# A hash-attention and gated-FFN kernel: batch 1 loaded and prepared early, the 1/32 moved into the copies from PSUM, V casts tied to bits, and a norm moved

## The chip, the core and the metric

The kernel runs on one core of a Trainium2 chip. The metric is the device time of one execution in microseconds (us); of several executions the median is given. TensorE (PE, with its weight loads shown as PEld), VectorE (DVE), ScalarE (ACT), GpSimd (POOL) and SyncE (SP) each work through their own instruction list in order and wait for one another through semaphores. DMAs move data between main memory, SBUF (the on-chip memory) and, here, also from one place of SBUF to another. PE writes its results to PSUM, from which ACT and DVE copy them out.

## The reference, cut to what matters

```python
# q, k, v: (4, 8, 768, 64); proj: (64, 6); x below: (3072, 512)
q_bits, k_bits = (q @ proj > 0), (k @ proj > 0)
mask = bucket(q_bits)[:, :, :, None] == bucket(k_bits)[:, :, None, :]
scores = where(mask, q @ k.T / sqrt(64), -1e9)
attn = softmax(scores)                    # with 1e-9 added to the sum
x = heads_side_by_side(attn @ v)
xn = x / sqrt(mean(x * x) + 1e-6) * rms_g
g = xn @ w_gate
out = (g * sigmoid(g) * (xn @ w_val)) @ w_out
```

A query sees only those keys whose six hash bits equal its own.

## The kernel before, in words

**Mask by arithmetic.** Each pair of heads of a batch has one tile `qk` of 71 rows: rows 0 to 63 hold the head dimensions in f16, scaled by 1/32 (`DIM`), rows 64 to 69 hold the hash bits as +0.5 or -0.5, row 70 a constant. One matmul over 71 rows thus gives score and bit agreement together, and `exp` with scale 128 makes the weight of a pair with unequal bits vanish. The constant rows are written once into each of six rotating `qk` tiles (`const_rows`).

**Preparing a pair of heads** (`make_prep`). `load_qk` and `load_v` issue the DMAs on SP's queue into rings of four buffers. `tr_mm` j transposes q (j = 0, 2) or k (j = 1, 3) on PE, three 128x128 blocks each, into a PSUM tile of the pool `ring` (four buffers); `tr_ev` copies it to SBUF, on ACT for q and DVE for k. `hash_mm` multiplies with proj for all four (query or key, head) combinations, `bits` compares with zero on DVE, and eight `place` DMAs of 4.5 KB, issued by SP, carry the bits to rows 64 to 69 of `qk`. `dims` writes rows 0 to 63, by the engine given ("a", "v" or "p" for GpSimd). The first two pairs of batch 0 (A and Bp; the others are C and Dp) write most bits straight from PSUM (`hash_one`, `direct`). `vcast` turns V into f16 and `vsum` adds up V for the 1e-9 term, both on GpSimd unless said otherwise.

**Attention** (`queue_attention`). u = 0 to 7 counts half-batches: batch u // 2, and the first or second half of its queries. Each u has 24 slots (8 heads of 3 key blocks): two score matmuls, two exponentials on ACT, and, 1.5 slots later, six matmuls with V (`pv`). Every six slots `post` divides by the sums on DVE; it reads the one accumulator tile `pv`, so the next `pv` group waits for it. After slot 23 `sumsq` squares and sums x, one call for each of the three token blocks.

**Norm and FFN**, one half-batch behind attention. `queue_norm`: `rstd` (one DVE operation and a power on GpSimd), `scale` (xn, three DVE operations), then `tr`, twelve f16 transposes on PE in two groups, and two copies to `xnT`, one on DVE and one on ACT. `queue_gates`: twelve blocks of eight matmuls, with tanh on ACT and two multiplications on DVE. `queue_out`: six groups of six matmuls, two half-batches behind attention.

**What sets the order.** Every step is given to `at` with a position, in units of a slot from the start of u = 0, and the list is emitted in order of position (lines 635 and 636). Each engine then sees its own part of that list, in that order, and takes it as its operands become ready: the position is no time, and an engine that is early in its list runs ahead until something that it needs is missing. `base` is the position of the half-batch in which a batch is prepared: 24, 72 and 120 for batches 1, 2 and 3. Pairs 0 and 1 of a batch are prepared in that half-batch, pairs 2 and 3 in the next.

## Time and profile before

| what | value |
|---|---|
| median of 3 runs | 379.11 us (377.8 to 380.17) |
| the profiled execution | 377.56 us |
| its span, first to last instruction | 375.8 us |
| PE busy | 348.1 us, 93% of the span |
| DVE, ACT, POOL busy | 236.6, 241.0, 83.9 us |
| mean clock granted to PE | 0.990 |
| first scores of u=0 | at 11.59 us |
| first output matmul (position 48.15) | at 81.04 us |
| moved by DMA | 31.2 MB, 83 GB/s over the span |

Times are read from the start of the span. Busy time is the union of an engine's instructions; the ends of matmuls are modelled, so a busy PE may still hold short gaps. A wait "A <- B" is time in which A's engine stood idle before A, ended by B. L182 is line 182 of the kernel. All of the prediction's rows are of this one execution.

### The profile page before, as it was taken

Reading aid. Unit: us, or ns where it says so; the run is one execution under the profiler, and the core shown is the slowest. Engines: PE = TensorE matmul, PEld = TensorE weight load, DVE = VectorE, ACT = ScalarE, POOL = GpSimd, SP = SyncE. Lnnn points to the kernel's source line nnn. Section 1 sums busy time; section 2 is a strip of 40 time slices with the busy share of each in tenths; the row PEclk is TensorE's granted clock in tenths of the full one; section 3 lists DMA queues with packets and bytes.
Section 4 is the critical chain, followed back from the end, with each engine's and each line's share of the span. In section 5 each row is a group of like instructions: output and inputs, shape, how many; then the busy total and the mean of one; then the engine's idle time right before and its main releaser. Section 6 shows DMA issues by size and latency. Waiting matters only on the chain.

```text
span 375.8 us, 7954 instructions
## 1 busy us (share of the span) xinstructions
PE 348.1 (93%) x3056; PEld 211.6 (56%) x3056; DVE 236.6 (63%) x475; ACT 241.0 (64%) x548; POOL 83.9 (22%) x106
## 2 busy tenths in 40 slices
PE   4887699999999989999999989999999999997995
PEld 3455366565656646565656646666565656663552
DVE  5776556758566684766746586566837565466670
ACT  3678766676767657676767656776676766872331
POOL 5999765200000292000000083200000000000000
PEclk9999889999999999999999999999999999999999
DMA  7702999900008503200004804200001000200202
GB/s 271 261 3 28 247 276 239 236 4 3 3 5 273 191 5 129 87 3 2 4 4 151 315 2 128 89 5 0 6 3 64 25 0 2 86 2 0 85 2 84
DMA packets 23846, 31.20 MB, mean 83 GB/s; under 512 B 1992, under 2 KB 20608, under 8 KB 23808
## 3 DMA queue, kind: packets, MB, share of 16 engines
q1 hardware_dynamic: 17824, 25.97, 20.5%
q0 software_dynamic: 5824, 4.72, 8.1%
q8 instruction: 24, 0.39, 0.4%
q14 instruction: 14, 0.11, 0.1%
q10 hardware_dynamic: 160, 0.00, 0.0%
HBM read 28.58 MB, written 6.29 MB: 93 GB/s over the span
## 4 chain that ended last, share of the span: by engine, by line
PE 53%; issue 25%; DVE 10%; POOL 5%; DMA 3%; ACT 3%; POOLq 0%; SPq 0%; DVEq 0%; ACTq 0%
PE v_ps L447 12%; PE g_ps L447 11%; PE o_ps L497 9%; PE s_ps L301 9%; PE pv L331 5%; PE trps L182 4%; POOL qk L241 3%; PE hps L195 2%; DVE qk L239 2%; DMA ql<-in_q_dram 2%; DVE sq L360 2%; DVE xn L395 2%; DMA kl<-in_k_dram 1%; ACT p L308 1%; ACT xnT L416 1%
## 5 line engine op out<-in xcount | busy, mean ns | idle before, releaser
L308 ACT ACTIVATE p<-s_ps 128x384 f16<-128x384 f32 x384 | 162.7, 496 | 70.6 <-PE s_ps L301 70.5
L301 PE MATMUL s_ps<-qk 71*128 71x384 f16 x384 | 95.7, 328 | 1.6 <-DVE qk L221 1.2
L464 DVE SCALAR_TENSOR_TENSOR a<-th,g_ps 128x384 f32<-128x384 f32 x96 | 53.1, 554 | 48.9 <-ACT th L456 47.7
L447 PE MATMUL g_ps<-xnT,wg 128*128 128x384 f16 x384 | 79.2, 325 | 4.2 <-ACT xnT L416 2.5
L447 PE MATMUL v_ps<-xnT,wv 128*128 128x384 f16 x384 | 78.0, 326 | 3.2 <-DVE a L464 3.2
L331 PEld LDWEIGHTS <-p 128*128 128x128 f16 x1152 | 60.2, 98 | 30.3 <-issue 8.9
L497 PE MATMUL o_ps<-wo,ht 128*128 128x512 f16 x288 | 68.7, 379 | 0.0
L331 PE MATMUL pv<-v,p 128*128 128x65 f16 x1152 | 67.9, 194 | 0.5
L456 ACT ACTIVATE th<-g_ps 128x384 f32<-128x384 f32 x96 | 47.8, 498 | 20.3 <-PE g_ps L447 17.3
L473 DVE TENSOR_TENSOR ht<-a,v_ps 128x384 f16<-128x384 f32 x96 | 53.0, 552 | 8.2
L388 POOL TENSOR_TENSOR rs<-ms,mhalf 128x3 f32<-128x3 f32 x8 | 6.9, 862 | 225.7 <-DVE ms L384 225.7
L447 PEld LDWEIGHTS <-wv 128*128 128x128 f16 x384 | 37.5, 98 | 29.2 <-issue 4.8
L447 PEld LDWEIGHTS <-wg 128*128 128x128 f16 x384 | 35.2, 97 | 26.1 <-issue 6.7
L497 PEld LDWEIGHTS <-ht 128*128 128x128 f16 x288 | 27.0, 97 | 27.4
L301 PEld LDWEIGHTS <-qk 71*128 71x128 f16 x384 | 28.4, 99 | 9.9 <-issue 1.3
L508 ACT ACTIVATE osb<-o_ps 128x512 f32<-128x512 f32 x23 | 13.7, 598 | 24.8 <-PE o_ps L497 24.8
L191 DVE COPY kT<-trps 128x384 f32<-128x384 f32 x32 | 17.7, 553 | 12.8 <-PE trps L182 12.6
L346 DVE RECIPROCAL r<-pv 128x6 f32<-128x6 f32 x32 | 6.2, 194 | 27.7 <-PE pv L331 27.7
L395 DVE SCALAR_TENSOR_TENSOR xn<-x,rs,grow 128x512 f16<-128x512 f32 x24 | 19.6, 869 | 5.6 <-POOL rs L388 5.6
L182 PE MATMUL trps<-ident,ql 128*128 128x128 f32 x96 | 17.7, 297 | 5.6 <-DMA ql<-in_q_dram 5.6
L189 ACT ACTIVATE qT<-trps 128x384 f32<-128x384 f32 x32 | 15.8, 493 | 10.9 <-PE trps L182 8.6
L182 PE MATMUL trps<-ident,kl 128*128 128x128 f32 x96 | 17.3, 292 | 1.7 <-DMA kl<-in_k_dram 1.4
(55 smaller groups left out, 280.5 us busy)
## 6 DMA issues: line engine op xcount, KB each, us to landing
ql<-in_q_dram SPq DMA_DIRECT2D x16, 384.0 KB
kl<-in_k_dram SPq DMA_DIRECT2D x16, 384.0 KB
vl<-in_v_dram SPq DMA_DIRECT2D x16, 384.0 KB
out_dram<-osb SPq DMA_DIRECT2D x7, 768.0 KB
qk<-bits SPq DMA_DIRECT2D x116, 4.5 KB
wg<-in_moe_w_gate_dram POOLq DMA_DIRECT2D x4, 384.0 KB, 13.6
wv<-in_moe_w_val_dram POOLq DMA_DIRECT2D x4, 384.0 KB, 17.0
wo<-in_moe_w_out_dram POOLq DMA_DIRECT2D x4, 384.0 KB, 24.7
```

The costliest lines, as they stand in the source:

```text
L182: nc.tensor.transpose(m[:, i, :], src[:, i, :], ident)
L189: nc.scalar.activation(dst, mm, AF.Copy)
L191: nc.vector.tensor_copy(dst, mm)
L301: nc.tensor.matmul(s_ps, qk[0:71, 2 + hh, 128 * jt : 128 * jt + 128], qk[0:71, hh, HQ * hf : HQ * hf + HQ], start=True, stop=True,)
L308: nc.scalar.activation(p, s_ps, AF.Exp, scale=SCL)
L331: nc.tensor.matmul(acc[:, t, hh, :], p[:, 128 * t : 128 * t + 128], v16s[b % 2][:, 2 * (jt % 3) + jt // 3, h, :], start=False, stop=(n % 6 ...
L395: nc.vector.scalar_tensor_tensor(out=tl["xn"][:, t, :], in0=x_of[u][:, t, :], scalar=tl["rs"][:, t : t + 1], in1=grow, op0=ALU.mult, op1=A ...
L447: nc.tensor.matmul(ps, w[:, kt, fs], xnT[:, kt, :], start=(kt == 0), stop=(kt == 3))
L456: nc.scalar.activation(th, tl[f][0], AF.Tanh, scale=0.5)
L464: nc.vector.scalar_tensor_tensor(out=a, in0=th, scalar=1.0, in1=g_ps, op0=ALU.add, op1=ALU.mult)
L473: nc.vector.tensor_mul(ht_of[u][f], a, v_ps)
L497: nc.tensor.matmul(tl[t], ht_of[u][f][:, 128 * t : 128 * t + 128], wo[:, f, :], start=(f == 0), stop=(f == 11),)
```

## The change

Seven edits, all to order and form; what is computed stays the same.

- **proj** is loaded once, after ACT's table load and warm-up, and DVE copies it to the other places that need it. A's transposes come in the order q, q, k, k instead of q, k, q, k.
- **The 1/32** is applied when q and k are copied from PSUM (`tr_ev`), on ACT or DVE; `dims` becomes a plain copy on all three engines. The sign of the hash product doesn't change by it.
- **Batch 1 early.** q and k of its pairs 0 and 1 are loaded at positions 1.5 and 4.2 (22 and 27 before), pairs 2 and 3 at 12.5 and 13.5. Pair 0 is prepared from 16.5 (28.4 before), inside u=0, and pair 1 from 32.3 (34.3). Both have all four evictions on DVE. The last two `const_rows` move from 26 and 27 to 12.6 and 12.7.
- **V loads and casts.** For batches 2 and 3 each V load, cast and sum stands after the bits (and so the placements) of a pair: pairs 0 and 1 after the bits of pair 0, pairs 2 and 3 after those of pair 1. For batch 1 they are at 30 to 36.3. Everywhere the hash comes 0.3 slot later.
- **Squares** of u=0 and u=7 are summed in two parts, 384 columns before the last `post` and 128 after it, and the parts added.
- **Norm transposes** come 5.2 slots behind the norm's start in u=0 (8.0 before), 3.7 in the others (4.1) and 5.0 for the last.
- **Around them:** the gates of u=0 start at 31 with a spacing of 1.42 (34.2 and 1.13 before); some bit placements of batch 0 that only the second half of the queries needs go behind others, one eviction of Bp goes to ACT, and the first gate weights are issued at 13.0 and 13.1 (12.1 and 12.2).

```diff
@@ -83,11 +83,10 @@
     pj = const.tile([128, 32], FP32, name="pj")
     nc.vector.memset(pj, 0.0)
-    nc.scalar.dma_start(out=pj[0:64, 0:6], in_=proj)
-    nc.scalar.dma_start(out=pj[64:128, 6:12], in_=proj)
     warm = const.tile([128, 1], FP32, name="warm")
     nc.vector.memset(warm, 0.0)
     nc.scalar.activation(warm, warm, AF.Exp)
+    nc.scalar.dma_start(out=pj[0:64, 0:6], in_=proj)
     ident = const.tile([128, 128], FP32, name="ident")
     make_identity(nc, ident)
     NQK = 6
@@ -112,10 +111,10 @@
     for e in range(2):
         t = const.tile([128, 32], FP32, name=f"pj1_{e}")
         nc.vector.memset(t, 0.0)
-        nc.vector.tensor_copy(
-            t[64 * e : 64 * e + 64, 0:6], pj[64 * e : 64 * e + 64, 6 * e : 6 * e + 6]
-        )
         pj1.append(t)
+    for e in range(2):
+        nc.vector.tensor_copy(pj1[e][64 * e : 64 * e + 64, 0:6], pj[0:64, 0:6])
+    nc.vector.tensor_copy(pj[64:128, 6:12], pj[0:64, 0:6])
     load_qk(0, 1)
     load_v(0, 0)
     load_qk(0, 2)
@@ -135,7 +134,7 @@
         vsums.append(t)
     const_rows(3, nc.gpsimd)
     for i in range(4, NQK):
-        at(22.0 + i, lambda i=i: const_rows(i, nc.gpsimd))
+        at(12.2 + 0.1 * i, lambda i=i: const_rows(i, nc.gpsimd))
     ident16 = const.tile([128, 128], FP16, name="ident16")
     nc.vector.tensor_copy(ident16, ident)
@@ -186,9 +185,9 @@
             dst = tl["qk"[j % 2]][:, j // 2, :]
             mm = tl.pop(("m", j)).rearrange("p c d -> p (c d)")
             if (eng or "av"[j % 2]) == "a":
-                nc.scalar.activation(dst, mm, AF.Copy)
+                nc.scalar.activation(dst, mm, AF.Copy, scale=DIM)
             else:
-                nc.vector.tensor_copy(dst, mm)
+                nc.vector.tensor_scalar_mul(dst, mm, DIM)
         def project(lhs, m):
             for c in range(4):
@@ -234,11 +233,11 @@
             dst = qk[0:64, 2 * c : 2 * c + 2, HQ * e : HQ * e + HQ]
             src = tl["qk"[c]][64 * e : 64 * e + 64]
             if eng == "a":
-                nc.scalar.activation(dst, src, AF.Copy, scale=DIM)
+                nc.scalar.copy(dst, src)
             elif eng == "v":
-                nc.vector.tensor_scalar_mul(dst, src, DIM)
+                nc.vector.tensor_copy(dst, src)
             else:
-                nc.gpsimd.tensor_scalar_mul(dst, src, DIM)
+                nc.gpsimd.tensor_copy(dst, src)
         def vcast(eng=None):
             vl = vloads[(b, hp)]
@@ -265,26 +264,26 @@
     PLACES = [(0, 0), (2, 0), (2, 1), (1, 0), (3, 0), (3, 1), (0, 1), (1, 1)]
-    def queue_prep(b, hp, p0, step, vp):
+    def queue_prep(b, hp, p0, step, hlag=0.3, eng=None):
         part = make_prep(b, hp)
-        part(vp, "vcast")
-        part(vp + 0.01, "vsum")
         for j in range(4):
             part(p0 + step * j, "tr_mm", j)
-            part(p0 + step * j, "tr_ev", j)
-        part(p0 + step * 4, "hash_mm")
-        part(p0 + step * 4, "bits")
+            part(p0 + step * j, "tr_ev", j, eng)
+        ph = p0 + step * 4 + hlag
+        part(ph, "hash_mm")
+        part(ph, "bits")
         for i, (c, e) in enumerate(PLACES):
-            part(p0 + step * 4 + 0.001 * (i + 1), "place", c, e)
+            part(ph + 0.001 * (i + 1), "place", c, e)
         for i, (c, e) in enumerate([(0, 0), (1, 0), (1, 1), (0, 1)]):
-            part(p0 + step * (4.2 + 0.3 * i), "dims", c, e)
+            part(ph + step * (0.2 + 0.3 * i), "dims", c, e)
+        return part, ph
     scores_of = {}
     probs_of = {}
     pv_of = {}
     x_of = {}
-    rs_of = {}
+    ss_of = {}
     def queue_attention(u, base, step, late):
         b, hf = divmod(u, 2)
@@ -351,16 +350,20 @@
                 )
             return go
-        def sumsq(t):
+        def sumsq(t, part, lo, hi):
             def go():
                 if t == 0:
-                    rs_of[u] = work.tile([128, 3], FP32, name="ss", tag="ss")
-                xs = x_of[u][:, t, :]
+                    ss_of[u, part] = work.tile([128, 3], FP32, name="ss", tag=f"ss{part}")
+                xs = x_of[u][:, t, lo:hi]
                 sq = work.tile([128, DMODEL], FP32, name="sq", tag="sq", bufs=1)
                 nc.vector.tensor_tensor_reduce(
-                    out=sq, in0=xs, in1=xs, scale=1.0, scalar=0.0,
-                    op0=ALU.mult, op1=ALU.add, accum_out=rs_of[u][:, t : t + 1],
+                    out=sq[:, lo:hi], in0=xs, in1=xs, scale=1.0, scalar=0.0,
+                    op0=ALU.mult, op1=ALU.add, accum_out=ss_of[u, part][:, t : t + 1],
                 )
+                if t == 2 and part == 1:
+                    s = work.tile([128, 3], FP32, name="ss", tag="ss2")
+                    nc.vector.tensor_add(s, ss_of[u, 0], ss_of[u, 1])
+                    ss_of[u, 0] = s
             return go
         for n in range(SLOTS):
@@ -369,9 +372,14 @@
             at(base + step * (n + lag), pv(n))
             if n % 6 == 5:
                 at(base + step * (n + lag + 0.05), post(n // 6))
+            split = DMODEL - 128 if u in (0, NU - 1) else DMODEL
+            if n == 17 and split < DMODEL:
+                for t in range(3):
+                    at(base + step * (n + lag + 1.0), sumsq(t, 0, 0, split))
             if n == 23:
                 for t in range(3):
-                    at(base + step * (n + lag + 0.06), sumsq(t))
+                    lo, part = (split, 1) if split < DMODEL else (0, 0)
+                    at(base + step * (n + lag + 0.06), sumsq(t, part, lo, DMODEL))
     xnT_of = {}
@@ -382,7 +390,7 @@
         def rstd():
             ms = work.tile([128, 3], FP32, name="ms", tag="ms")
             nc.vector.tensor_scalar(
-                ms, rs_of[u], 1.0 / DMODEL, 1e-6, op0=ALU.mult, op1=ALU.add
+                ms, ss_of[u, 0], 1.0 / DMODEL, 1e-6, op0=ALU.mult, op1=ALU.add
             )
             rs = work.tile([128, 3], FP32, name="rs", tag="rs")
             nc.gpsimd.tensor_tensor(rs, ms, mhalf, op=ALU.pow)
@@ -525,9 +533,9 @@
     A, Bp, C, Dp = [make_prep(0, hp) for hp in range(4)]
-    for j in range(4):
-        A(-24.0 + j, "tr_mm", j)
-        A(-24.0 + j, "tr_ev", j)
+    for i, j in enumerate((0, 2, 1, 3)):
+        A(-24.0 + i, "tr_mm", j)
+        A(-24.0 + i, "tr_ev", j)
     Bp(-20.5, "tr_mm", 0)
     A(-20.0, "dims", 0, 0, "a")
     A(-19.9, "dims", 1, 0, "a")
@@ -537,7 +545,7 @@
     A(-19.3, "dims", 1, 1, "a")
     Bp(-19.2, "tr_mm", 1)
     Bp(-19.1, "tr_ev", 0)
-    Bp(-19.0, "tr_ev", 1)
+    Bp(-19.0, "tr_ev", 1, "a")
     A(-18.1, "dims", 0, 1, "p")
     A(-18.0, "vcast")
     A(-18.0, "vsum")
@@ -572,7 +580,7 @@
     C(7.6, "hash_mm")
     C(7.6, "bits")
     for i, (c, e) in enumerate(PLACES):
-        C(7.61 + 0.01 * i, "place", c, e)
+        C((7.61 if e == 0 or c > 1 else 12.0) + 0.01 * i, "place", c, e)
     for i, (c, e) in enumerate([(0, 0), (1, 0), (1, 1)]):
         C(7.9 + 0.1 * i, "dims", c, e, "ppv"[i])
     C(8.3, "vcast", nc.vector)
@@ -583,49 +591,70 @@
     Dp(11.4, "hash_mm")
     Dp(11.4, "bits")
     for i, (c, e) in enumerate(PLACES):
-        Dp(11.41 + 0.01 * i, "place", c, e)
-        if i == 5:
-            for cc in range(2):
-                A(11.461 + 0.001 * cc, "place", cc, 1)
-                Bp(11.463 + 0.001 * cc, "place", cc, 1)
+        Dp((11.41 if e == 0 or c > 1 else 12.2) + 0.01 * i, "place", c, e)
+    for i, P in enumerate((A, Bp)):
+        for c in range(2):
+            P(12.1 + 0.01 * c + 0.02 * i, "place", c, 1)
     for i, (c, e) in enumerate([(0, 0), (1, 0), (1, 1)]):
         Dp(13.7 + 0.3 * i, "dims", c, e, "v")
     Dp(12.8, "vcast", nc.vector)
     Dp(11.5, "vsum")
     for i, P in enumerate((Bp, C, Dp)):
-        P(15.0 + 1.0 * i, "dims", 0, 1)
+        P(14.8 + 0.6 * i, "dims", 0, 1)
     for c in range(4):
         for wh in range(2):
-            at((12.1 if c == 0 else 13.0) + 0.1 * (2 * c + wh), lambda c=c, wh=wh: load_gv(c, wh))
+            at(13.0 + 0.1 * (2 * c + wh), lambda c=c, wh=wh: load_gv(c, wh))
     for c in range(4):
         at(26.0 + 2.0 * c, lambda c=c: load_wo(c))
+
+    def qk_at(pos, b, hp):
+        at(pos, lambda: load_qk(b, hp))
+
+    def v_at(pos, part, b, hp):
+
+        at(pos, lambda: load_v(b, hp))
+        part(pos + 0.3, "vcast")
+        part(pos + 0.31, "vsum")
+
+    qk_at(1.5, 1, 0)
+    qk_at(4.2, 1, 1)
+    qk_at(12.5, 1, 2)
+    qk_at(13.5, 1, 3)
     for b in range(1, B):
         base = SLOTS * (2 * b - 1)
+        if b == 1:
+            p0s = (16.5, 32.3, base + SLOTS + 0.4, base + SLOTS + 8.3)
+        else:
+            p0s = (base + 0.4, base + 10.3, base + SLOTS + 0.4, base + SLOTS + 8.3)
+            for hp in range(4):
+                qk_at(base - 8.0 + 5.0 * hp, b, hp)
+        parts = [
+            queue_prep(b, hp, p0s[hp], 1.0, eng="v" if b == 1 and hp < 2 else None)
+            for hp in range(4)
+        ]
+        if b == 1:
+            vps = [base + 6.0 + 2.0 * hp for hp in range(4)]
+        else:
+            vps = [parts[hp // 2][1] + 0.1 + 1.5 * (hp % 2) for hp in range(4)]
         for hp in range(4):
-            early = 8.0 if b == 1 else 0.0
-            at(base - 8.0 + 5.0 * hp + 0.75 * early, lambda b=b, hp=hp: load_qk(b, hp))
-            at(base - 3.0 + 3.5 * hp + early / 2, lambda b=b, hp=hp: load_v(b, hp))
-            p0 = base + (0.4, 10.3, SLOTS + 0.4, SLOTS + 8.3)[hp]
-            if b == 1 and hp == 0:
-                p0 += 4.0
-            queue_prep(b, hp, p0, 1.0, base + 8.5 + 3.5 * hp)
+            v_at(vps[hp], parts[hp][0], b, hp)
     for u in range(NU):
         queue_attention(u, SLOTS * u, 1.0, 1.1 if u == 0 else 0.0)
         p = SLOTS * (u + 1) + 0.6
         if u == 0:
-            queue_norm(u, p, 1.0, 8.0)
+            queue_norm(u, p, 1.0, 5.2)
         else:
-            queue_norm(u, p, 1.0, 4.1)
+            queue_norm(u, p, 1.0, 3.7 if u < NU - 1 else 5.0)
     F = SLOTS / 18.0
     steps = lambda base, js: [base + 0.15 + F * j for j in js]
     for u in range(NU):
         base = SLOTS * (u + 1)
         if u == 0:
-            queue_gates(u, [base + 10.2 + 1.13 * j for j in range(12)], 1.13)
+            queue_gates(u, [base + 7.0 + 1.42 * j for j in range(12)], 1.42)
         else:
             js = [4, 5, 6, 7, 10, 11, 12, 13, 14, 15, 16, 17] if u < NU - 1 else range(6, 18)
             queue_gates(u, steps(base, js), F, u == NU - 1)
```

## The prediction

> **What bounds the kernel now.** I read the page's busy table first, then the waits of PE, then the busy time by stretch, then the order of instructions where a stretch was poor. The page's first row, and the clock row of the 40 slices:
>
> ```profile
> PE 348.1 (93%) x3056; PEld 211.6 (56%) x3056; DVE 236.6 (63%) x475; ACT 241.0 (64%) x548; POOL 83.9 (22%) x106
> ...
> PEclk9999889999999999999999999999999999999999
> ```
>
> PE is the bound, and no PE work is removed: what can be won is the 27.7 us in which PE is idle (375.8 - 348.1) and the work done at the low clock. The list of PE's waits, and the stretches (span, busy PE, PEld, DVE, ACT, POOL, clock, DMA):
>
> ```profile
> PE trps L182 <- DMA ql<-in_q_dram: 5.6, 2, 3.9
> ...
> PE xtp L408 <- DVE xn L395: 1.9, 3, 1.2
> ...
> PE pv L318 <- POOL vsum L256: 1.3, 1, 1.3
> ```
>
> ```profile
> 40.00:50.00 10.00, 7.76 (x61) 5.35 (x62) 5.66 (x14) 6.08 (x16) 6.46 (x10) 0.70 1.21 269
> 43.50:44.00 0.50, 0.00 (x0) 0.00 (x0) 0.50 (x1) 0.00 (x0) 0.50 (x1) 0.90 1.19 278
> 50.60:51.00 0.40, 0.40 (x9) 0.28 (x7) 0.36 (x1) 0.00 (x0) 0.40 (x1) 0.84 1.15 265
> 84.00:128.00 44.00, 42.95 (x387) 26.38 (x385) 28.56 (x60) 29.84 (x69) 0.88 (x1) 1.00 0.30 101
> 128.00:172.00 44.00, 42.07 (x379) 25.87 (x378) 29.25 (x56) 29.67 (x68) 13.83 (x17) 1.00 0.14 48
> ```
>
> See two things. The first stage of batch 1 waits for q at 44.1 us (one of the two ql waits; the other, 3.9, is the start), and the clock is half from 43.9 to 50.7 (from the two partial slices: 6.8 us). The stage with GpSimd busy (128 to 172) loses 0.9 us of PE more than the one without. The order of instructions says why; start, duration, engine:
>
> ```profile
> 44.13 0.87 PE L182 MATMUL trps<-ident,ql 128*128 128x128 f32 x3 [1.77 <-DMA ql<-in_q_dram]
> ```
>
> ```profile
> 87.24 2.08 DVE L395 SCALAR_TENSOR_TENSOR xn<-x,rs,grow 128x512 f16<-128x512 f32 x3 [0.54 <-POOL rs L388]
> 89.24 0.55 DVE L191 COPY kT<-trps 128x384 f32<-128x384 f32 x1
> ...
> 130.24 3.56 DVE L395 SCALAR_TENSOR_TENSOR xn<-x,rs,grow 128x512 f16<-128x512 f32 x3 [0.51 <-POOL rs L388]
> 133.72 0.55 DVE L191 COPY kT<-trps 128x384 f32<-128x384 f32 x1
> ```
>
> The same three xn take 2.08 us alone and 3.56 beside the V casts; kT is queued behind them, and the hash matmul waits for kT.
>
> **Start (about +0.3 us).** The proj load moves behind the table load: before, its two DMAs were issued at 0.92 and 1.50 us, and the copy of the second ran at 6.41, 4.9 us later. The one now left is issued near 2.4 (0.92 + 1.28 table load + 0.20 warm-up), so it lands between 5.9 and 7.3. Behind it on VectorE stand three copies (0.17 each) and 0.46 us of constants, then the two kT evictions (0.56 each), then the first hash, at 8.93 before. Landing at 7.3 gives 9.35, at 5.9 gives 8.25, because k is now transposed second and third in row and its evictions could start at 7.08. I take +0.3, bounds -0.7 and +1.5 (a DMA two microseconds later than the later row). One eviction of the second pair goes to ScalarE, which waited 0.85 us after it in any case; ScalarE's three dims become copies, a form the trace lacks: I keep its 0.84, and 0.5 to 1.0 changes nothing, since the first scores waited for VectorE's bits.
>
> **First half-batch, u=0.** GpSimd's six dims took 2.12 to 2.50 us each as TENSOR_SCALAR; as copies the nearest row is its own V cast, 128x768 in 0.83 us (bounds 0.5, a GpSimd add of 128x128, and 2.12). Six times 1.3 saves 8 us of GpSimd, which was 95% busy from 10 to 40 us. That takes away PE's waits of 1.33 (vsum at 31.1) and 0.28 (dims at 28.2), but ScalarE is the bound there: from 31.85 its exponentials run back to back, 22 in 8.54 us, 0.39 each, 0.78 a slot against about 0.51 for PE. So I credit 0.3 us. The 1/32 in the evictions costs nothing: TENSOR_SCALAR from PSUM takes 0.558 (bits) and COPY 0.553. The q bits of the second half (c = 0, 1 with e = 1) are placed after D's first six: SP issues one per 0.7 us, so A's go out near 34 us and are read from slot 24, near 38: hidden, and 1 us if not.
>
> **The early prep of (batch 1, heads 0-1).** Its q and k wait only for A's transposes (done by 10.7 us) and land by about 20, needed near 31: the 1.77 us wait is gone, and with it the cause of the 6.8 us at half clock (worth up to 3.4 us). Its PE work, 4 x 0.4 transposes and 0.8 hash, moves into slots where PE has 0.27 us a slot to spare. But VectorE is in order, and now carries, from the end of pv 11 (29.5 us: 29.47 before, +0.3, -0.3): post 0.76, six dims 3.2, four evictions 2.24, post 0.76, three part sums 3 x 0.61 = 1.83 (512 columns cost 0.74 start to start, 0.53 of it columns), bits 0.56, four dims 2.1. Sum 11.45: it reaches the last post of u=0 at 40.95, where that post ran at 39.22. This is what is late next. From there post 0.8, three short sums 1.0, two small operations 0.35, the power on GpSimd 1.0, xn 2.08: xn is ready at 46.2, and the norm transposes, now 5.2 slots behind, not 8, stand on PE's queue before everything else and wait for it until 46.4.
>
> After that PE has 18 slots of 0.51, 12 gates of 1.3, one prep of 2.4, norm transposes 0.8 and bias matmuls 0.5: 28.5 us. Before, 28.4 us of such work took from 50.78 to 81.04, 30.3 with its small stalls. So slot 48 comes at 76.7 against 81.04. PE idles over 2 us near 40 and over 1 us near 45, and the row above shows the clock halved after 1.77 us of idle; the cost lies between 0 and 3.4 us (6.8 at half), I take 1.5, nearest to the middle since only part of such a stretch would be dense. Net -2.8. Bounds: -5.8 (VectorE not late; the transposes then wait for ScalarE's slots until 44.9, no half clock) and +2.2 (VectorE's ten dims each 0.3 slower as beside vsum in 30.6 to 32.7, xn 3 us later, half clock in full).
> The Trainium skill ("TensorE: Matmul & The Clock Gate", Part 1) says the clock falls back after an idle window of about 3.4 us; the trace shows it falling after 1.77 us without a matmul. By the page the 1.5 us would be 0, and the sum 1.5 lower.
>
> Gate weights: issued 33.7 to 39.4 before, landing 5.7 to 25.5 us later; now GpSimd reaches them near 29. First needed near 47, last near 69: hidden, and if not, each of four chunks would stop PE outright.
> A rule that speaks against this: "SBUF - State Buffer", "Who interferes with whom", has GpSimd and VectorE copies between SBUF operands exclude each other, and "SBUF: two separate sides" lets that starve GpSimd's DMA issues. The eight issues (0.77 to 0.81, the first 1.28) now lie beside VectorE's dims; by the page, an estimate of 8 x 0.5 = 4 us later, still inside that cover: sum unchanged.
>
> **Stages u=2 to u=7.** The norm transposes move 0.4 slot forward, ahead of pv and hash. In u=2 PE ended the output matmuls before them at 89.75 and xn was ready at 89.3: margin 0.45 us. The gate's second half of xnT then starts about 92.55, not 93.14 (ScalarE's copy, 0.82, overlaps a scores pair): -0.6 in u=2, 4, 6, -0.5 in u=7. In u=3 and u=5 the V loads now stand in SP's queue behind eight bit placements (about 5.7 us), so the casts come after xn: from the end of the output matmuls to that point u=3 took 4.83 us, u=2 3.39, so -1.4 more each. 3 x 0.6 + 0.5 + 2 x 2.0 = 6.3; I take 5.8, bounds 3 and 7. Casts then lie beside gate work, where a VectorE operation took 0.56 beside GpSimd at 139.05, as without it.
>
> **End, u=7.** Chain from the last post to the gates:
>
> ```profile
> 338.84 0.20 DVE L346 RECIPROCAL r<-pv 128x6 f32<-128x6 f32 x1 [0.91 <-PE pv L331]
> ...
> 343.06 2.08 DVE L395 SCALAR_TENSOR_TENSOR xn<-x,rs,grow 128x512 f16<-128x512 f32 x3 [1.03 <-POOL rs L388]
> ...
> 343.87 0.28 PE L408 MATMUL xtp<-ident,xn 128*128 128x128 f16 x2 [1.18 <-DVE xn L395]
> ```
>
> PE waits 1.18 + 0.38 + 0.38 = 1.94. The sums shrink from 2.2 to 1.0, plus one add 0.15, so xn ends at 344.1; one more output block (1.3) stands before the transposes, so PE is busy to 344.0. Gates start near 346.0, not 348.24: -2.2 (bounds -1.2, -2.4). The part sums fall where VectorE is half idle.
>
> **Sum.** The +0.3 of the start and the -0.3 of u=0 are inside the 29.5, so: -2.8 - 5.8 - 2.2 = -10.8. The profiled execution took 377.56 (span 375.8), so 366.8; it lies 1.5 below the median 379.11, and I put the new median half of that above the sum: **367.5 us**. Of this kernel about 1% can be told from no change.
>
> **Rivals.** (1) VectorE is not late and the clock holds: -5.8 instead of -2.8: 364.5. For it: ScalarE, not VectorE, paced that stretch before. Chance 0.22. (2) VectorE's queue and the half clock eat the whole gain of batch 1: +2.2, about 372.5. For it: dims at 1.04 us beside GpSimd in this trace; against: GpSimd is through with its sums by then. 0.13. (3) The load does not come early, because its buffers or SP's queue hold it: the wait and half clock stay, 377.6 - 5.8 - 2.2 + 0.7 = 370. The loads stand ahead of all placements, so 0.05. (4) Slower: the norm transposes, earlier by 0.4 slot, outrun xn in all six stages u=2 to u=7 and stop PE so long that the clock halves each time: 1.8 idle + 3.4 = 5.2 each, 31 us, less 5 gained: 404. It decides from xn 0.45 + 1.77 = 2.2 us late; the worst lateness in the trace is 1.48. 0.05. The forecast has 0.55.
>
> The range 362 to 374 takes in rivals 1 to 3 and the bounds of the start. Faster by over 1% 0.88, within 1% 0.06, slower 0.06.
>
> **What would show it.** Right: no ql wait after the start; u=0's last post near 41; norm transposes waiting for xn near 46; the first gates near 47, not 54; xn near 2.1 us for three in u=3 and u=5; gates of u=7 some 2.2 us after one short transposes stop. Wrong: PE waiting for wg or wv, an xn wait in each stage, or a start with the first scores after 12.5 us (11.59 now).

## Result and the profile after

The changed kernel takes 366.39 us (median of four runs, 365.18 to 367.13) against 379.04 us before on the same chip: ratio 0.9664, 95% interval 0.9621 to 0.9707. The profiled execution took 366.99 us with a span of 365.2. The forecast was 367.5 us. The total is right and lies in the range, but its two large terms are both wrong, in opposite directions, as the trace shows.

The first row of the page of the changed kernel (busy time of each engine) and the clock row of the 40 slices:

```profile
PE 346.3 (95%) x3056; PEld 212.7 (58%) x3056; DVE 238.5 (65%) x493; ACT 239.2 (66%) x545; POOL 70.9 (19%) x106
...
PEclk9998799899999999999999999999999999999999
```

PE's work is the same 3056 matmuls; its idle time fell from 27.7 to 18.9 us. GpSimd fell by 13 us. The clock is no longer down in one place but in two.

The list of PE's waits in the changed kernel (total us, times, longest):

```profile
PE trps L181 <- DMA ql<-in_q_dram: 3.8, 1, 3.8
...
PE g_ps L455 <- ACT xnT L424: 1.9, 7, 0.4
PE v_ps L455 <- DVE a L472: 1.7, 1, 1.7
PE trps L181 <- DVE qT L190: 1.1, 1, 1.1
PE g_ps L455 <- DVE ht L481: 1.0, 1, 1.0
PE xtp L416 <- DVE xn L403: 0.8, 3, 0.4
```

The wait for q of batch 1 is gone: the one that is left is the start of the kernel. So are vsum and the 1.9 us for xn at the end. Three waits of a microsecond or more are new, one each, all for VectorE.

Each window below is a stretch of the changed kernel; the columns are span and busy time of PE, PEld, DVE, ACT and POOL, with the number of instructions in brackets, then granted clock, DMA share and GB/s:

```profile
30.23:33.64 3.41, 1.97 (x24) 1.31 (x23) 3.41 (x6) 2.64 (x7) 3.41 (x6) 1.00 1.15 137
33.64:37.05 3.41, 3.13 (x22) 2.04 (x20) 1.94 (x5) 1.38 (x4) 1.12 (x2) 0.50 1.32 204
37.05:40.47 3.42, 3.24 (x24) 1.43 (x25) 2.66 (x9) 0.82 (x3) 0.00 (x0) 0.50 1.32 204
...
64.36:67.77 3.41, 1.50 (x18) 1.01 (x18) 3.35 (x6) 0.87 (x2) 3.25 (x5) 1.00 0.66 108
67.77:71.18 3.41, 3.38 (x14) 1.66 (x14) 2.10 (x4) 0.80 (x2) 3.17 (x6) 0.50 0.02 4
```

```profile
84.00:128.00 44.00, 43.73 (x399) 27.62 (x398) 29.31 (x61) 30.88 (x71) 0.88 (x1) 1.00 0.23 74
128.00:172.00 44.00, 43.76 (x404) 27.73 (x403) 29.88 (x63) 31.33 (x72) 11.99 (x18) 1.00 0.22 74
```

The first fence holds the two stretches at half clock, 6.82 and 3.41 us long, each behind a window in which VectorE and GpSimd were full and PE was not. The second shows the steady stages: PE is busy 43.73 and 43.76 of 44 us, where it was 42.95 and 42.07, and the stage with GpSimd busy now loses nothing against the other.

One division makes everything after this readable. The first output matmul of u=0 (slot 48) divides the span:

| | before | after | change | forecast |
|---|---|---|---|---|
| start to first output matmul | 81.04 | 82.54 | +1.5 | -2.8 |
| from there to the end of the span | 294.76 | 282.66 | -12.1 | -8.0 |

The second part hardly varies: 282.63 to 282.68 in eight traces of kernels that keep it as it is in the changed kernel (spans are printed to 0.1 us), and 283.18 in a ninth. That one has the same times up to the output matmuls of u=7, the last thing that PE does, and 11.99 us from their start to the end where the others have about 11.5. The kernel before has 11.96 there, so some 0.5 of the 12.1 us is a difference at the very end that comes and goes between traces. Up to the output matmuls of u=7 the gain is 11.61 (282.80 to 271.19). A single trace is enough to measure an edit in this part. The first part differs by microseconds from one execution to the next, and needs timed runs.

### The profile page after: what moved, and what is told of

Same layout as the page of the kernel before. It is cut to its first block, busy times and chain, and to the rows that moved or that the text cites. A ratio compares the mean times of both kernels' runs of the same rounds, so it can differ in the third digit from the quotient of the medians.

```text
span 365.2 us, 7966 instructions
## 1 busy us (share of the span) xinstructions
PE 346.3 (95%) x3056; PEld 212.7 (58%) x3056; DVE 238.5 (65%) x493; ACT 239.2 (66%) x545; POOL 70.9 (19%) x106
## 4 chain that ended last, share of the span: by engine, by line
PE 87%; DVE 7%; ACT 3%; issue 1%; DMA 1%; POOL 0%; ACTq 0%; DVEq 0%; POOLq 0%
PE v_ps L455 17%; PE g_ps L455 17%; PE o_ps L505 16%; PE s_ps L300 15%; PE pv L330 9%; PE trps L181 6%; PE hps L194 4%; DVE qk L238 2%; PE xtp L416 2%; ACT xnT L424 2%; PE pv L317 1%; DVE xn L403 1%; DVE x L346 1%; DMA ql<-in_q_dram 1%; DVE sq L359 1%
## 5 line engine op out<-in xcount | busy, mean ns | idle before, releaser
L472 DVE SCALAR_TENSOR_TENSOR a<-th,g_ps 128x384 f32<-128x384 f32 x96 | 53.2, 554 | 46.2 <-ACT th L464 44.9
L464 ACT ACTIVATE th<-g_ps 128x384 f32<-128x384 f32 x96 | 48.0, 500 | 19.1 <-PE g_ps L455 16.5
L300 PEld LDWEIGHTS <-qk 71*128 71x128 f16 x384 | 28.4, 99 | 12.7 <-issue 4.7
L190 DVE TENSOR_SCALAR kT<-trps 128x384 f32<-128x384 f32 x31 | 17.2, 553 | 12.5 <-PE trps L181 12.4
L244 POOL CAST v<-vl 128x768 f16<-128x768 f32 x14 | 12.0, 857 | 64.0 <-PE trps L181 27.1
L403 DVE SCALAR_TENSOR_TENSOR xn<-x,rs,grow 128x512 f16<-128x512 f32 x24 | 16.6, 748 | 5.6 <-POOL rs L396 5.6
L188 ACT ACTIVATE qT<-trps 128x384 f32<-128x384 f32 x28 | 13.8, 494 | 7.8 <-PE trps L181 7.6
```

What stands on the lines that cost most here:

```text
L190: nc.vector.tensor_scalar_mul(dst, mm, DIM)
L300: nc.tensor.matmul(s_ps, qk[0:71, 2 + hh, 128 * jt : 128 * jt + 128], qk[0:71, hh, HQ * hf : HQ * hf + HQ], start=True, stop=True,)
L403: nc.vector.scalar_tensor_tensor(out=tl["xn"][:, t, :], in0=x_of[u][:, t, :], scalar=tl["rs"][:, t : t + 1], in1=grow, op0=ALU.mult, op1=A ...
L464: nc.scalar.activation(th, tl[f][0], AF.Tanh, scale=0.5)
L472: nc.vector.scalar_tensor_tensor(out=a, in0=th, scalar=1.0, in1=g_ps, op0=ALU.add, op1=ALU.mult)
```

## Experiments: the second part

Four kernels, each the changed kernel with one thing undone and run once; only the time from the first output matmul to the end is compared.

**V casts untied** (cast_untied): loads, casts and sums of V of batches 2 and 3 at their old positions.

```diff
-            vps = [parts[hp // 2][1] + 0.1 + 1.5 * (hp % 2) for hp in range(4)]
...
+                at(base - 3.0 + 3.5 * hp, lambda b=b, hp=hp: load_v(b, hp))
+                parts[hp][0](base + 8.5 + 3.5 * hp, "vcast")
+                parts[hp][0](base + 8.51 + 3.5 * hp, "vsum")
```

> The changed kernel with the V loads, casts and sums of batches 2 and 3 at the fixed positions that they had before, ahead of the bits' placements. To read: the time from the first output matmul of u=0 to the end of the span (294.8 us before, 282.7 in the changed kernel) and the lengths of the stages. Theory A (the forecast's term): u=3 and u=5 get 1.4 us longer each, so 285.5. Theory B: all of what these two stages gained more than their neighbours (2.77 against 1.10) is the casts, 1.67 each: 286.0. Theory C: with the norm's earlier place the casts disturb nothing: under 283.2.

Measured: 285.86, so the tie is worth 3.20 us, 1.6 for each of u=3 and u=5 (forecast 1.4): nearer to theory B (286.0) than to A (285.5). The order of instructions of this kernel in u=3 shows the same 3.56 us for three xn as before; in the changed kernel the line reads 2.08:

```profile
132.74 3.56 DVE L403 SCALAR_TENSOR_TENSOR xn<-x,rs,grow 128x512 f16<-128x512 f32 x3 [0.51 <-POOL rs L396]
```

```profile
130.64 2.08 DVE L403 SCALAR_TENSOR_TENSOR xn<-x,rs,grow 128x512 f16<-128x512 f32 x3 [0.51 <-POOL rs L396]
```

**Norm transposes back to 4.1 slots** (gap41), u=1 to u=6:

```diff
-            queue_norm(u, p, 1.0, 3.7 if u < NU - 1 else 5.0)
+            queue_norm(u, p, 1.0, 4.1 if u < NU - 1 else 5.0)
```

> The changed kernel with the norm transposes of u=1 to u=6 back at 4.1 slots after the norm (3.7 in the changed kernel), u=7 left. To read: the same time from the first output matmul to the end of the span (282.7 us in the changed kernel). Theory A (the forecast's term): 0.6 us for each of five stages and 0.5 for the sixth: 286.2. Theory B: all of the gain of the even stages is this: 1.1 for each of five and 0.45 for u=7, about 288.6. Theory C: the gain of the even stages comes from the cheaper copies and the moved V work, and the gap is worth under 0.2 a stage: below 284.

Measured: 286.14, so 3.48 us: theory A, the forecast's 0.6 a stage to the hundredth (the first half of u=2, from the first to the fifth output block, is 20.85 us here and 20.26 in the changed kernel). Theory B fails: something else gave the even stages another 0.5 us each.

**The end as before** (tail_whole): u=7's squares in one part, its norm transposes at 4.1.

```diff
-            queue_norm(u, p, 1.0, 3.7 if u < NU - 1 else 5.0)
+            queue_norm(u, p, 1.0, 3.7 if u < NU - 1 else 4.1)
...
-            split = DMODEL - 128 if u in (0, NU - 1) else DMODEL
+            split = DMODEL - 128 if u == 0 else DMODEL
```

> The changed kernel with u=7 as before: the squares summed in one part behind the last post and the norm transposes at 4.1 slots, not 5.0. To read: the time from the first output matmul to the end of the span (282.7 us in the changed kernel). Theory A (the forecast's term): 2.2 us longer, 284.9. Theory B: what the last stage gained in all, 2.8 us, 285.5. Theory C: the output block that now stands ahead of the transposes hid the wait alone, without the shorter sums: under 1 us.

Measured: 285.02, so 2.36 us (forecast 2.2). The three together explain 9.0 of 12.1 us.

**The hash matmul a slot behind the transposes** (hlag0): the change also puts every hash 0.3 slot later. The diff shows it in one default argument, and the forecast gave it no price. Bits, placements and dims stand relative to the hash, and so do the V loads and casts of batches 2 and 3, so in this experiment they move with it.

```diff
-            queue_prep(b, hp, p0s[hp], 1.0, eng="v" if b == 1 and hp < 2 else None)
+            queue_prep(b, hp, p0s[hp], 1.0, eng="v" if b == 1 and hp < 2 else None,
+                       hlag=0.3 if b == 1 and hp < 2 else 0.0)
```

> The changed kernel with the hash matmul of every head pair prepared in u=2 to u=6 back at a whole slot after the last transposes, where it stood before (it stands 0.3 slot later in the changed kernel). To read: the time from the first output matmul to the end of the span (294.8 us before, 282.7 in the changed kernel; 286.1 with the norm's gap undone, 285.9 with the V casts undone, 285.0 with the tail undone, which leaves about 3.0 of the 12.1 without a cause). Theory A: these 0.3 slots, which the forecast did not price, are that rest: about 285.5. Theory B: the rest comes from the cheaper copies on VectorE and GpSimd: 282.7, as in the changed kernel.

Measured: 285.77, so 3.11 us: theory A. PE's waits of this kernel from 84 to 330 us:

```profile
PE v_ps L455 <- DVE a L472: 2.3, 5, 0.7
PE g_ps L455 <- ACT xnT L424: 1.5, 6, 0.2
```

In the changed kernel the first of these lines is missing for that stretch. The kernel before had the same 2.3 us there (0.3 us in an even stage, 0.6 in an odd one). VectorE's instructions around the second hash of u=2, first of this kernel, then of the changed one:

```profile
109.39 0.56 DVE L205 TENSOR_SCALAR bits<-hps 128x384 f16<-128x384 f32 x1 [2.08 <-PE hps L194]
...
110.33 0.18 DVE L345 RECIPROCAL r<-pv 128x6 f32<-128x6 f32 x1
...
112.63 0.56 DVE L472 SCALAR_TENSOR_TENSOR a<-th,g_ps 128x384 f32<-128x384 f32 x1
```

```profile
106.93 0.20 DVE L345 RECIPROCAL r<-pv 128x6 f32<-128x6 f32 x1 [1.43 <-PE pv L330]
...
107.77 0.56 DVE L205 TENSOR_SCALAR bits<-hps 128x384 f16<-128x384 f32 x1
...
110.33 0.55 DVE L472 SCALAR_TENSOR_TENSOR a<-th,g_ps 128x384 f32<-128x384 f32 x1
```

At the old place, VectorE idles 2.08 us for the hash and the post of pv stands behind bits, so `a` of the next gate comes 2.88 us after the gate's first matmul (109.75). With 0.3 slot more the post goes ahead, into that idle time, and `a` comes 2.39 us after it (107.94). The halves of the stages say the same: with the old place the second half of u=2 takes 22.18 us (22.18 before, 21.67 after) and that of u=3 22.94 (22.95 before, 22.22 after).

The four add up: 3.48 + 3.20 + 3.11 + 2.36 = 12.15 of 12.10 us; up to the output matmuls of u=7 3.45 + 3.14 + 3.01 + 2.29 = 11.89 against 11.61, so they overlap by no more than 0.3. The cheaper copies of the 1/32 edit have no share in this part.

## Experiments: the first part

**Early preparation of batch 1 undone** (late_b1), with the place of u=0's norm and gates; the evictions of its q go back to ScalarE too:

```diff
-    qk_at(1.5, 1, 0)
-    qk_at(4.2, 1, 1)
-    qk_at(12.5, 1, 2)
-    qk_at(13.5, 1, 3)
...
-            p0s = (16.5, 32.3, base + SLOTS + 0.4, base + SLOTS + 8.3)
+            p0s = (base + 4.4, base + 10.3, base + SLOTS + 0.4, base + SLOTS + 8.3)
...
+            qk_at(base - 8.0 + 5.0 * hp + (6.0 if b == 1 else 0.0), b, hp)
...
-            queue_norm(u, p, 1.0, 5.2)
+            queue_norm(u, p, 1.0, 8.0)
...
-            queue_gates(u, [base + 7.0 + 1.42 * j for j in range(12)], 1.42)
+            queue_gates(u, [base + 10.2 + 1.13 * j for j in range(12)], 1.13)
```

> The changed kernel with the early preparation of batch 1 undone: loads of q and k, the transposes and hashes of its first two head pairs, and the norm and gates of u=0 stand where they stood before; all else stays changed. Theory A (two errors of the forecast cancelled): the early preparation did not pay 2.8 us but cost some 3 us, because VectorE's longer queue and the V casts halve the clock twice; without it the first output matmul comes near 79.7 us (81.04 before, less the 1.35 us that the start gained), 2.8 us sooner than in the changed kernel, and the median is near 363.6 us. Theory B (the forecast's reading): the early preparation pays, so the wait for q of 1.8 us and the half clock of some 7 us come back and the median is near 369 us. Between, at 366 to 367: the early preparation is worth nothing either way.

Measured: 366.77 us, ratio to the kernel before 0.9648 (0.9598 to 0.9698), the same as the changed kernel's 0.9664. Neither A nor B: the early preparation is worth nothing that can be measured, either way. The trace of this kernel has 17 us at half clock (34.1 to 51.1), where the changed kernel has 6.8 and 3.4 us, and still has its first output matmul at 80.96. Its clock fell at 34.1 us without the wait for batch 1's q eviction, so that wait is not the only thing that brings the clock down there. What the early preparation removes, it pays for elsewhere.

**Where it pays.** In the changed kernel VectorE is late twice. Its instructions from 28 to 34 us, and those near 62 us (start, duration, operation):

```profile
28.59 0.54 DVE L238 CAST qk<-qT 64x768 f16<-64x768 f32 x1
29.05 1.64 DVE L238 CAST qk<-kT 64x768 f16<-64x768 f32 x2
30.62 2.30 DVE L238 CAST qk<-qT 64x768 f16<-64x768 f32 x3
32.85 0.53 DVE L190 TENSOR_SCALAR qT<-trps 128x384 f32<-128x384 f32 x1
...
61.79 0.54 DVE L238 CAST qk<-qT 64x768 f16<-64x768 f32 x1
62.25 2.54 DVE L238 CAST qk<-kT 64x768 f16<-64x768 f32 x1
```

Six dims stand ahead of the eviction of batch 1's q, and PE waits 1.06 us for it at 33.44. At 62.25 one CAST takes 2.54 us instead of 0.54: GpSimd is at that time casting and summing V of batch 1 (this work runs from 58.91 to 71.9 us), and the value matmuls then wait 1.70 us for `a`. Behind each stands a stretch at half clock in this trace; start_old (below) has a CAST of 2.13 us at 64.45 and no half clock behind it.

Three kernels moved these. **v1_early** sets the V work of batch 1 earlier in the order:

```diff
-            vps = [base + 6.0 + 2.0 * hp for hp in range(4)]
+            vps = [base + 2.4 + 1.7 * hp for hp in range(4)]
```

> The changed kernel with the V loads, casts and sums of batch 1 some four slots earlier (positions 26.4 to 31.5, not 30 to 36), so that GpSimd is done or nearly done when VectorE writes the four dims of (batch 1, heads 2-3). Theory A: the dims CAST that took 2.54 us beside GpSimd takes near 0.55, the waits of 1.70 us (v_ps for a) and 0.99 us (g_ps for ht) go, and with them the half clock of 3.2 us (1.6 us): 3 to 4 us less, median near 363. Theory B: the dims are slow for another reason, or PE is held there by ScalarE anyway: under 0.7 us less, median 365.7 to 367.

Measured: 368.76 us, ratio 0.9695 (0.9654 to 0.9736): no gain, and above what both theories gave. The collision did not go: in this trace PE waits 1.4 us for `a` and 2.4 us for `ht`. The transfers from 34 to 60 us run at 242 GB/s on average, GpSimd waits 11.5 us for V, and its casts run from 56.26 us, through the dims again: one CAST of 2.13 and one of 2.60 us. An earlier place in the order is no earlier place in time.

**dims_moved** takes some 4 us of dims out of VectorE's way in u=0:

```diff
-        P(14.8 + 0.6 * i, "dims", 0, 1)
+        P(17.2 + 0.6 * i, "dims", 0, 1, "p")
...
+                       dlag=6.0 if b == 1 and hp == 0 else 0.2)
```

> The changed kernel with VectorE relieved in u=0: the three dims of the second half's q of heads 2 to 7 go to GpSimd at positions 17.2 to 18.4, and the four dims of (batch 1, heads 0-1) run after xn of u=0; a fourth qT buffer makes room, and the throw-away output of the squares is BF16 for it. Theory A: VectorE's lateness causes the wait of 1.06 us for the qT eviction at 33.4 us and the 6.4 us at half clock behind it; without some 4 us of dims ahead of the last post, the last post of u=0 comes near 39.5 us (42.84), the clock stays at 1, and the median is 2 to 4 us lower, near 363.5. Theory B: ScalarE's exponentials set the pace of u=0 anyway, PE stays sparse and the clock falls all the same: under 1 us, median 365.4 to 367.

Measured: 366.85 us, ratio 0.9651 (0.9610 to 0.9691). The last post came at 39.07 and the stall near 33 us went, as theory A says. But the clock did not stay at 1: it fell at 44.56 us and, behind the collision near 62 us, which stayed, at 65.04. There is no gain that can be told from none; the number is theory B's, but ScalarE's pace as its reason is not shown.

**both_moves** joins them, V work at positions 28 to 33:

> Both moves together (the V work of batch 1 at positions 28 to 33). Theory A: the two stalls are separate places and the gains add, 5 to 7 us: first output matmul near 76.5 us (82.54 in the changed kernel; the forecast said 78.2 in the profiled execution), median near 360.5. Theory B: what is freed in u=0 is given back in u=1, where PE then waits for something else: no lower than the better of the two alone.

Measured: 364.34 us, ratio 0.9574 (0.9530 to 0.9618). Better than either alone (its interval just touches that of dims_moved), but not by the 5 to 7 us that theory A gave: the V casts run from 59.70 us, the dims near 62 us take 0.60 to 1.35 us each, and the first output matmul comes at 79.27.

**v_loads_first** loads V before q and k of heads 4 to 7, so that the casts can run early, and puts the second pair's first transposes behind the first hash:

```diff
-    Bp(-20.5, "tr_mm", 0)
+    Bp(-19.7, "tr_mm", 0)
...
-    qk_at(12.5, 1, 2)
-    qk_at(13.5, 1, 3)
+    for hp, pos in enumerate((5.0, 10.0, 12.5, 13.5)):
+        at(pos, lambda hp=hp: load_v(1, hp))
+    qk_at(24.0, 1, 2)
+    qk_at(30.0, 1, 3)
```

> Both moves of dims and V casts, and two more: V of batch 1 is loaded into its buffers as they come free (positions 5 to 13.5) and q and k of its heads 4 to 7 only at 24 and 30, since the transfers between 31 and 60 us run at some 270 GB/s and brought V late, so that the casts ran at 60 us whatever their place in the order; and the second pair's first transposes stand behind the first hash, not ahead of it, where they kept it waiting for their load by 0 to 1.7 us. Theory A: the casts end before the dims of (batch 1, heads 2-3) near 62 us, no wait of VectorE for GpSimd over 1 us is left there, the first output matmul comes near 77.5 us; 3.5 to 5 us below the changed kernel. Theory B: the weights now land later and PE waits for wg or wv in u=0's gates, or a wait for q at 24: no better than the changed kernel.

Measured: 365.83 us, ratio 0.9667 (0.9625 to 0.9708): no better than the changed kernel that can be told, but for neither reason given. With their data there, the casts ran as soon as GpSimd had the power behind it, at 44.40 us, beside xn of u=0, and the dims behind it:

```profile
42.90 4.17 DVE L403 SCALAR_TENSOR_TENSOR xn<-x,rs,grow 128x512 f16<-128x512 f32 x3 [1.08 <-POOL rs L396]
46.99 0.81 DVE L238 CAST qk<-qT 64x768 f16<-64x768 f32 x1
47.73 1.90 DVE L238 CAST qk<-kT 64x768 f16<-64x768 f32 x2
```

The collision had moved from 62 to 43 us, and 10.2 us at half clock with it. That speaks for late V work, not early.

**v_tied** does that: V loads of batch 1 behind the bit placements of its heads 2 and 3 in SP's queue, as the change itself does for batches 2 and 3, with the moves of dims and of the first hash kept.

```diff
-            vps = [base + 6.0 + 2.0 * hp for hp in range(4)]
+            vps = [parts[1][1] + 1.2 + 1.5 * hp for hp in range(4)]
```

> The moves of dims in u=0 as before, the second pair's first transposes behind the first hash, and the V loads of batch 1 in SP's queue behind the eight bit placements of (batch 1, heads 2-3), as the change does for batches 2 and 3: positions 37.8 to 42.3. The casts can then run neither beside xn (where they made it 4.17 us for three in the last version, 2.08 without) nor beside the dims near 62 us. Expected: V casts from about 69 us on, dims of 0.55 to 0.6 us each, no wait of PE for VectorE over 0.7 us between 58 and 80 us, xn 2.08. Theory A (VectorE beside GpSimd is what costs in both places): ratio to the kernel before 0.948 to 0.956, first output matmul near 78 us, clock at 1 from 44 us on. Theory B: the clock falls after short stalls in any case, or vsum of heads 0 and 1 is late for u=2: ratio 0.957 or more.

Measured: **360.71 us**, ratio to the kernel before 0.9520 (0.9474 to 0.9566): faster than both kernels, and in theory A's range. Its longest waits of PE, over the whole span, and VectorE near 59 us:

```profile
PE trps L181 <- DMA ql<-in_q_dram: 3.9, 1, 3.9
PE pv L317 <- DVE x L346: 3.4, 5, 0.9
PE g_ps L455 <- ACT xnT L424: 1.5, 6, 0.2
PE g_ps L455 <- DVE xnT L422: 1.0, 1, 1.0
```

```profile
58.61 0.55 DVE L205 TENSOR_SCALAR bits<-hps 128x384 f16<-128x384 f32 x1
59.07 0.54 DVE L238 CAST qk<-qT 64x768 f16<-64x768 f32 x1
59.54 0.54 DVE L238 CAST qk<-kT 64x768 f16<-64x768 f32 x1
...
60.57 0.56 DVE L238 CAST qk<-kT 64x768 f16<-64x768 f32 x1
61.05 0.55 DVE L238 CAST qk<-qT 64x768 f16<-64x768 f32 x1
```

All four dims take 0.54 to 0.56 us, the V casts run from 68.13 us, the trace has no half clock between the start and the last matmul, and the first output matmul comes at 75.34 us (78 expected), near the forecast's own best case for the change (81.04 - 5.8 = 75.24). The spans of all six executions less 282.7 us give a first part of 75.2 to 77.5 us; the three longer ones have a mean clock of 0.988 to 0.995, so the clock still falls in some executions. The gain that the forecast gave to the early preparation is there to be had.

Which of the three moves brought it is not shown one by one. The nearest pair is v_loads_first, which has the same moves of dims and hash: it differs in when batch 1's V and the q and k of its heads 4 to 7 are loaded, and in the casts behind them. Its ratio is 0.9667 against 0.9520, the intervals are apart, and in neither trace does PE wait for those q and k. So the late V work is the likely cause. GpSimd and VectorE still meet elsewhere in v_tied: two dims at 28.72 us take 0.82 us each beside the issue of the gate weights.

**The start** (start_old): proj loads, copies and the order of the first transposes as before.

```diff
+    nc.scalar.dma_start(out=pj[0:64, 0:6], in_=proj)
+    nc.scalar.dma_start(out=pj[64:128, 6:12], in_=proj)
...
-    for i, j in enumerate((0, 2, 1, 3)):
+    for i, j in enumerate((0, 1, 2, 3)):
```

> The changed kernel with its start as before: two loads of proj, copies in place, q and k transposed in turns, the second pair's k evicted by VectorE. Theory A: the start gained some 1.2 us because the one proj load is issued at 0.94 us in any case and the copies no longer wait for a second load: the copies end after 6.3 us (5.2 in the changed kernel), the first hash comes near 8.9 us (7.3), the first scores near 11.5 us (10.2). Theory B: the first scores depend on when q and k of the first two pairs land, which differs from execution to execution by more than a microsecond (9.9 to 11.4 us in the four kernels that kept the new start); the old start gives 10 to 10.6 too.

Measured: first hash at 8.93, first scores at 11.85 us; the changed kernel's are at 7.32 and 10.24. Theory A for this one trace, but B is right about the spread. The new start gives its first scores at 9.80 to 10.32 us in five traces and at 11.35 to 12.08 us in five others. In all ten the second pair's transposes stand ahead of the first hash, and in the late ones they wait for their q by 0.6 to 1.7 us; both_moves:

```profile
8.70 0.52 PE L181 MATMUL trps<-ident,ql 128*128 128x128 f32 x3 [1.73 <-DMA ql<-in_q_dram]
9.15 0.52 PE L194 MATMUL hps<-qT,pj 128*32 128x384 f32 x2
```

The wait is not all of it: late_b1 waits 0.66 us there and has its first scores at 10.23, cast_untied waits 0.65 and has them at 11.35. In late_b1 the first hash matmuls take 0.52 us, in cast_untied 0.86, so when the clock rises at the start counts too. In the two kernels where those transposes stand behind the hash the first scores came at 9.92 and 10.39. start_old as a whole had its first output matmul at 80.32, before that of the changed kernel, with no half clock between the start and the last matmul: in these two traces 1.6 us of start weigh less than where the clock falls.

**The changed kernel again** (after_again):

> The changed kernel as it is, beside the version below on the same chip. From the first output matmul to the end of the span it takes 282.7 us again; the first output matmul itself comes anywhere between 80 and 85 us, as in the four executions whose first 80 us had the same program, for the half-clock stretches there differ from one execution to the next (1.7, 3.4 or 5.1 us lost to the clock). Theory A (the first part is nearly a draw in the median): ratio to the kernel before 0.964 to 0.969. Theory B (the forecast's 2.8 us are there in most executions): ratio below 0.962.

Measured: 367.80 us (365.86 to 370.33, six runs), ratio 0.9711 (0.9657 to 0.9764): nearest to theory A, 0.002 above the range that it gave. The span less 282.7 us gives the first part of each of the ten timed executions of the changed kernel: 80.7 to 85.8, mean 82.9 us. The kernel before, with 294.8 us for its second part (from its one trace) and 1.8 us around the span, gives 81.2 to 83.6, mean 82.4, for the four runs of the first comparison. Six traces whose program is the changed kernel's up to there have the first output matmul anywhere from 80.16 (gap41) to 85.82 (after_again). The first part is a draw: the whole gain of 12 us is the second part's. Nor does the mean clock alone order the times: the shortest of the first four executions (365.18 us) had the lowest one, 0.975.

## Why the prediction was right, and where it was wrong

**Start, "+0.3".** Wrong in its step. The load was put at 2.4 us "behind the table load", landing from 5.9 to 7.3. It was issued at 0.94 us, while the table load ran from 0.73 to 2.01: ScalarE's DMA issue does not stand behind it in the trace. The copies were over at 5.20 us and the first scores came 1.35 us earlier, beyond the bound of -0.7. The second loss was not seen at all: the order of transposes that puts the second pair ahead of the hash costs up to 1.7 us when its q lands late.

**First half-batch, "-0.3".** GpSimd's dims as copies took 0.82 us (forecast 0.83, against 2.12): the right row was taken. post of pv 11 came at 27.90 (29.5 given), 1.57 us sooner than before, about what the start gave.

**Early preparation, "-2.8, bounds -5.8 to +2.2".** This step failed: +1.5 in the profiled execution, nothing that the timed runs can tell. Its chain ran over the last post ("at 40.95"), xn ("ready at 46.2") and slot 48 ("76.7", without the 1.5 us for the clock). In the trace these came at 42.84 (39.22 before), 48.18 and 82.54. So of 5.8 us, some 1.8 were lost up to xn, and 4.1 behind it: 34.4 us from xn to slot 48, where the sum has 30.3.

Up to xn the queue of VectorE was right in kind, but priced at 11.45 us back to back; from 27.90 to 42.84 it took 14.94. The six dims took 4.3 us, not the "3.2" of the sum; in the trace of before they had taken 4.4 already (30.18 to 34.62). And VectorE stood waiting for PE, which had no term in the sum; these four rows hold 2.85 us of it:

```profile
34.23 0.56 DVE L190 TENSOR_SCALAR qT<-trps 128x384 f32<-128x384 f32 x1 [0.38 <-PE trps L181]
35.84 0.56 DVE L190 TENSOR_SCALAR kT<-trps 128x384 f32<-128x384 f32 x1 [1.05 <-PE trps L181]
...
39.55 0.56 DVE L205 TENSOR_SCALAR bits<-hps 128x384 f16<-128x384 f32 x1 [0.66 <-PE hps L194]
...
42.84 0.20 DVE L345 RECIPROCAL r<-pv 128x6 f32<-128x6 f32 x1 [0.76 <-PE pv L330]
```

PE was at half clock for most of that time. In v1_early, with the same dims and no half clock there, the last post came at 40.74 and xn was ready at 46.08, as forecast. Rival 2 (0.13) had the slow dims, and the counter-argument ("GpSimd is through with its sums by then") was beside the point: GpSimd was busy issuing the gate weights, 4.00 of 4 us from 30 to 34. The estimate of 4 us later for these issues did not come true: behind the first, 0.76 to 0.80 us each, as before; it was VectorE's dims that paid.

Behind xn the second collision, V casts of batch 1 against dims of its heads 2 and 3, had no term: the forecast looked for it in the odd stages from u=3 on and not in u=1, whose V casts the change does not tie to the bits. That this is the larger loss, two traces support: v1_early had xn on time and the collision, and its first output matmul came at 82.86, 36.8 us after xn; v_tied was free of it and took 30.85 us from xn (44.49) to slot 48, close to the forecast's 30.3.

**Stages, "3 x 0.6 + 0.5 + 2 x 2.0 = 6.3; I take 5.8, bounds 3 and 7".** Measured by the lengths of the stages: 1.10, 2.77, 1.11, 2.77, 1.11, 0.45, together 9.3, above the upper bound. 0.6 for the gap held to 0.01 us, the casts' 1.4 is 1.6. What is missing is the hash's 0.3 slot, 3.1 us (hlag0), which the forecast passed over. In the trace of before its place could have been seen: PE's wait for `a` is the second longest of the list, 3.2 us in seven times, and the forecast did not ask which operation stood ahead of `a`:

```profile
PE v_ps L447 <- DVE a L464: 3.2, 7, 0.6
```

**End, "-2.2".** 2.36. From the last post to the gates 7.10 us, where it was 9.40; the twelve transposes stand behind one more output block and wait no more:

```profile
330.83 5.34 PE L505 MATMUL o_ps<-wo,ht 128*128 128x512 f16 x24
336.01 0.99 PE L416 MATMUL xtp<-ident,xn 128*128 128x128 f16 x12
336.84 1.46 PE L505 MATMUL o_ps<-wo,ht 128*128 128x512 f16 x6
```

**Gate weights, hidden.** Right: no wait of PE for wg or wv in any of the traces. **Rivals 1, 3 and 4** did not happen: VectorE was late and the clock fell, the loads came early, and xn waits in the steady stages sum to 0.2 us.

So 366.8 + 0.7 met 366.4 by luck: one term (the early preparation) was 3 to 4 us too good and another (the stages) 3.5 us too small, and the two cancelled. A range that holds a total says nothing on its terms.

## What to carry to other kernels

Before work is moved to an earlier slot, list what the in-order engines do there and what runs beside it: here all that an early load gained went to a longer queue on VectorE and to GpSimd's casts beside its copies. Work on GpSimd is not made harmless by an earlier or later number in an order; tie it to an event (here: the loads behind the bits in SP's queue) that comes after the copies with which it collides. And read a diff for small constants: 0.3 slot in a default argument was worth 3.1 us, nearly as much as the norm's gap (3.5) or the tied casts (3.2), since it set which of two operations stood first in VectorE's queue.

## What the runs showed of the hardware

**The clock falls in steps of 3.41 us, on a fixed grid.** All stretches at half clock between the start and the last matmul of a trace are 3.41, 6.83, 10.24 or 17.07 us long: one, two, three or five steps of 3.413. In the changed kernel they begin at 33.64 and 67.77, ten steps apart; in dims_moved at 44.56 and 65.04, six steps apart. The Trainium skill ("TensorE: Matmul & The Clock Gate", Part 1) states a free-running window of 3413 ns, and these runs agree with it. They do not agree with its condition of an idle window: PE was never idle for a whole step. The step of the grid ahead of a fall had PE busy for 1.10 to 2.20 us in fifteen of the sixteen falls in these traces, and 2.49 in the other. The phase of the grid differs between executions, and it seems to have a part in what a stall costs; no run here sets it. v1_early has the same wait of 1.05 us at 33.5 as the changed kernel, and its steps there read:

```profile
28.44:31.85 3.41, 2.85 (x38) 2.25 (x39) 3.38 (x6) 3.13 (x9) 3.41 (x6) 1.00 0.45 37
31.85:35.26 3.41, 2.08 (x23) 1.39 (x22) 2.95 (x6) 1.93 (x5) 2.98 (x5) 1.00 1.31 203
35.26:38.68 3.42, 2.36 (x26) 1.09 (x26) 3.28 (x11) 1.61 (x5) 0.00 (x0) 1.00 1.32 205
```

Here 2.08 us of busy PE in a step did not bring the clock down, where 1.97 did in the changed kernel. A sharp threshold can't be read from this: both_moves fell after 2.15, and dims_moved after 2.49 where both_moves did not after 2.48. Ends of matmuls are modelled in these records, so the busy time is itself uncertain.

**VectorE and GpSimd between SBUF operands slow each other, by up to 2 us an instruction.** A 64x768 CAST on VectorE took 0.54 us alone and 0.60 to 1.38 beside work of GpSimd, and in nine of the traces one or two between 60 and 66 us took 2.13 to 2.61 beside GpSimd's casts and sums of V; three xn 2.08 alone, 3.56 and 4.17 beside them. A cast of V on GpSimd took 0.83 alone and up to 1.23. VectorE operations that read PSUM kept their 0.53 to 0.56 in the same stretches. The Trainium skill ("SBUF — State Buffer", "Who interferes with whom") describes a port pair that the two share; the runs agree, and add that here it is VectorE's copies, on PE's path, that pay for it.
